# Idle products on TensorE ahead of the first h, the first two x tiles as one DMA, and the last output tiles in column halves

## Chip, cores and metric

The kernel runs on one core of a Trainium2 chip. The metric is the device time in microseconds; the median of 8 runs of the kernel before is 255.04 us (253.82 to 255.74). Lower is better.

## What is computed

One transformer block with adaptive layer norm (adaLN), for one sequence of 2048 positions, width 512, all in bfloat16:

```python
mod = silu(c) @ w_mod                       # six vectors of 512: sa, ca, ga, sb, cb, gb
h = layernorm(x) * (1 + ca) + sa
q, k, v = split(h @ wqkv)                   # 32 heads of 16
# sliding, dilated attention: position s sees s, s-2, ..., s-14 (8 keys)
logits = einsum('bhsd,bhswd->bhsw', q, k_gathered) * 16 ** -0.5
o = einsum('bhsw,bhswd->bhsd', softmax(logits), v_gathered)
x = x + ga * (o @ wo)
h = layernorm(x) * (1 + cb) + sb
x = x + gb * ((silu(h @ w1) * (h @ w3)) @ w2)   # w1, w3: 512 x 1792, w2: 1792 x 512
```

## The kernel before

The sequence is cut into 16 tiles of 128 positions, named T in the code. Everything stays in SBUF but v and the attention weights, which go to DRAM scratch and come back shifted, so that the eight neighbours of a position lie in one partition each.

The kernel does not write its instructions in order. It declares operations (`p.op`, `p.dma`), each with an engine, an estimated cost, a key into a table of priorities, and the values that it reads and writes. `schedule` then goes through time and gives each free engine the ready operation with the lowest priority value; buffers come from pools (8 PSUM banks, 5 of xn, 3 of h, 2 of pq, 2 of vsh and one more, vshx, on top of wqkv, 2 of o). The outcome is one fixed order for each engine, and `synchronize` puts semaphore waits where an operation depends on another engine. So each engine works through a list in order: where the head of a list waits, everything behind it on that engine waits too. Nearly all DMAs are issued from SP, in the order that the planner gave them, and cT alone from ScalarE.

The steps that the change and the prediction touch, with their lines in the profile:

- **Loads** (L133 for every DMA). x tiles 0 and 1 are two DMAs of 128 KB, then w_mod's first part (1 MB), then tiles 2 and 3 as two DMAs, then wqkv in three parts (q, k, v; 512 KB each) and the remaining x in groups of four tiles.
- **Modulation** (`modulation`, L522 to L531): 32 products of w_mod with silu(c), then three small VectorE operations give the scale and shift that the first h needs.
- **Layer norm** (`ln_stats`, L550 to L558): VectorE statistics (L550, L551), rstd on GpSimd in two operations (L553, L555), and the normalized tile xn on VectorE (L558).
- **h** (`ln_T`): TensorE transposes xn (L574, with the constant `ident`), and ScalarE (L582), in two early groups also VectorE (L589), applies scale and shift. Tiles are taken in the groups of `LN1` (2, 2, 4, 4, 4) for the first norm and of `FFN` (2, 4, 4, 4, 2) for the second.
- **Projections**: q and k transposed (`proj_qk`, L615), v (`proj_v`, L633); ScalarE evicts them (L622, L623, L643).
- **Attention**: VectorE forms all products q * k of a tile (`pq`, L664, 128x4096); TensorE sums them over each head with `E_sb` (L673); ScalarE takes exp (L687); VectorE normalizes (L699 to L710); the weights go through DRAM; VectorE multiplies the shifted v, `vsh`, by them (L733, 128x4096); TensorE sums over the neighbours with `ind` (L742); L755 multiplies by wo and L759 adds to x.
- **FFN** (`ffn_unit`): gate and up products (L771), Silu on ScalarE (L777), the product of both on VectorE (L780); `ffn_w2` sums 14 products with w2 (L792), L798 adds x, and a DMA stores the tile.
- **Constants**: GpSimd sets `ident`, `cst`, `ones` (L440), `E_sb` and the rest.

FFN work of early tiles fills TensorE while later tiles are in attention; the planner decides where.

Of the kernel before, what the change touches and what calls it, by code (L numbers as in the profile page):

```python
# [8 lines left out]
ALU = mybir.AluOpType  # L9
AX = mybir.AxisListType  # L10

P = 128
S = 2048
D = 512
# [5 lines left out]
NT = S // P  # L20
KT = D // P
NF = F // P
# [6 lines left out]
LAT = {"sp": 1900, "pe": 230, "dve": 70, "act": 150, "pool": 120}  # L29
DMA_RATE = 350  # L30
# [53 lines left out]
class Program:  # L84
# [41 lines left out]
    def dma(self, out, in_, key, nbytes, r=(), w=(), part=(), after=(), eng="sp", cost=450, group=None):  # L126
        nc = self.nc

        def fn(e):
            a = out() if callable(out) else out  # L130
            b = in_() if callable(in_) else in_
            with nc.allow_non_contiguous_dma(reason="layout"):
                return e.dma_start(a, b)  # L133

        o = self.op(eng, fn, cost, key, r=r, w=w, part=part, after=after, dma=nbytes)
        if group is not None:
            group.append(o)
            o.group = group
        return o

    def schedule(self, prio):
# [25 lines left out]
        while len(self.placed) < len(ops):  # L167
# [10 lines left out]
            for e in ENGINES:  # L178
# [31 lines left out]
                if o.dma:  # L210
                    dma_free = max(busy[e], dma_free) + o.bytes // DMA_RATE
                    o.end = dma_free + LAT["sp"]
                else:
                    o.end = busy[e] + LAT[e]
# [109 lines left out]
def c_dve(n):  # L324
    return 140 + n * 25 // 24
# [4 lines left out]
VG = 2  # L330
LN1 = [[0, 1], [2, 3], [4, 5, 6, 7], [8, 9, 10, 11], [12, 13, 14, 15]]
# [3 lines left out]
def _build(p, A_x, A_wqkv, A_wo, B_w1, B_w3, B_w2, c, w_mod, out):  # L335
# [67 lines left out]
    def bank(v):  # L403
        return PALL[:, v.at * 512:(v.at + 1) * 512]
# [28 lines left out]
    k = ("const", 0)  # L433
    p.op("pool", lambda e: e.memset(ident[:], 0.0), 150, k, w=[vident])
# [5 lines left out]
    p.op("pool", lambda e: e.memset(ones[:], 1.0), 150, k, w=[vc])  # L440
# [21 lines left out]
    p.dma(bass.AP(cT, 0, [[KT, P], [1, KT]]), bass.AP(c.tensor, c.offset, [[1, P], [P, KT]]), ("load", 0), 1024, w=[vcT],  # L462
          eng="act")
    for T in range(4):
        p.dma(x_sb[:, T, :], x_view[:, T, :], ("load", 1 if T < 2 else 19), 131072, w=[vx[T]])
    p.dma(wm_s[0][:], wm_view[:, :, 0:1024], ("load", 2), 1048576, w=[vwms[0]])
# [46 lines left out]
    def modulation(i):  # L513
# [17 lines left out]
        p.op("dve", lambda e: e.tensor_copy(modc[:, jlo:jlo + 8], modc_bf[:, jlo:jlo + 8]), 180, k, r=[vb16], w=[vmod[i]])  # L531

# [253 lines left out]
    def ffn_w2(T, tt, vhh):  # L786
        vz = Val("ps_z", psum)
        o = None
        for q in range(2):
            def mm(e, q=q):  # L790
                for fi in range(7 * q, 7 * q + 7):
                    ins = e.matmul(bank(vz), vhh[fi].at[:, tt * P:(tt + 1) * P], w2[:, fi, :], start=(fi == 0),  # L792
                                   stop=(fi == NF - 1))
                return ins

            o = p.op("pe", mm, 7 * MM, ("z", 2 * T + q), r=vhh[7 * q:7 * q + 7] + [vw2s], part=[vz], after=[o] if q else [])
        vo = Val("o", opool)
        p.op("dve", lambda e: e.tensor_tensor(vo.at[:], bank(vz), x_sb[:, T, :], ALU.add), c_dve(512), ("zo", T),  # L798
             r=[vz, vx[T]], w=[vo])
        finals.append(p.dma(out2d[T * P:(T + 1) * P, :], lambda: vo.at[:], ("zo", T), 131072, r=[vo], cost=400))  # L800

    modulation(0)
# [36 lines left out]
def _priorities():  # L839

    return {
        "ac": [-200350, -305143, -144949, -247454, -248998, -144926, 118091, 153034, 127660, 128134, 144119, -511708, -511789, 144159, 233884,
            140161],
        "ad": [-17874, -30405, -32779, -22500, -24840, -32434, -28265, -27668, 1469, -27769, 384, 367, 2705, 132755, -1479, -1613],
        "al": [-26059, -18199, -29495, -32976, -260310, -30646, -28356, -25679, -27023, -29130, 662, 915, 2008, 137184, 1131, 135573],
        "av": [-237126, -167739, 117729, 116760, 129499, 127502, -3576, 163212, 134914, 166331, 224073, 159673, 234283, 170474, 234369, 175760],
        "const": [-318511, -250028],
        "ex": [-152588, -142436, -140021, 53300, -139876, 74900, 96361, 96500, 96599, 118100, 127701, 139700, 124737, 182900, 182900, 182900],
        "f": [-13079, -234848, -103997, -152504, -114086, -145296, -116384, -248184, -248481, -146619, -145234, -198977, 121830, -31495, -146237,
            114050, 113238, 127970, 128137, 118188, 147491, -15588, -145226, 97902, 150981, -105983, -114355, 110896, 128277, 166736, 235566, 145004,  # L850
            129095, 111421, 199964, 125683, 128614, 162509, 159600, 129622, 140758, 180049, 222333, 160180, 163223, 238682, 226292, -511536, 159927,
            145684, -524879, 162898, 227475, 160131, -524977, 180052, 232502, 199837, 199314, -520876, -529180, 317000, 199316, 226185, 232431,
            -531683, 232315, 171522, 232311, 321759],
        "k": [-322297, -572741, -198760, -190131, -154342, -255908, -243988, -543578, -127644, -154350, -149316, -575519, -330997, -235009, -148795,
            -28906, -145161, -149323, -146794, -17610],
        "lg": [-150634, -142803, -233180, -327164, -249257, -235004, -259981, 127075, -199338, 128790, 139453, -31273, 113254, 140864, 118136,
            116232],
        "load": [99478, -565364, -558539, -275990, -275913, -291765, -289165, -25490, -17320, -28263, -14185, -289174, -261975, -5041, -260002,
            -17585, -261281, -30733, -17861, -296743],
        "mod": [-148763, -253150, -235125, -124038, -322327, -22533, -249983, -148006, 123104],  # L860
        "nm": [-1510043, -243017, -251504, -237638, -150689, -231747, -258507, -243906, -1114132, -232706, -250945, -254085, -250939, -247676,
            -248814, -240438, -234864, -234850, 126758, -146950, 130896, 140866, 168836, 126007, 134932, 122376, 159389, 164928, 225919, 126136,
            234809, 224413],
        "pq": [-252871, -156171, -145021, -250929, 127472, -240380, -243423, -244902, -109341, -239613, 169717, -108539, 134008, 133814, 125253,
            121981],
        "q": [-197716, -152472, -543562, -208803, -191857, -208358, -154375, -239569, -326610, -543026, -38787, -29129, -52704, -305134, -18763,
            106892, 113215, 91084, -141122, -151034],
        "rs": [-240379, -244702, 123968, -170661, -980, 135729, 175752, 128124, 163815, 128591, 122384, 227742, 128453, 133854, 128526, 159856],
        "sm": [-252811, -147149, -243616, 55300, 114437, 76900, -241462, 98500, -103045, 120100, 135088, 141700, 211236, 163300, 226628, 184900],
        "st": [-936849, -506834, -232582, 101744, -247943, -254078, -146807, -247930, -149835, -254071, -254208, -242818, -248804, -147329, -251009,  # L870
            -242935, -244460, -240797, 135436, 134779, 128454, -146248, 168855, 169729, 169974, 129804, 224348, 237239, 180639, 135109, 127857,
            238854],
        "tr": [98770, -253363, -208119, -243937, -192255, -188054, -56370, -256934, -138446, -189820, -122575, -31488, -152236, -146560, 140966,
            140158, 166028, 120267, 229725, -516185],
        "v": [-543494, -542831, -191851, -325240, -135881, -575945, -200493, -154170, 114839, -146400, -259983, 118127, -147068, -6268, -31482,
            -4183],
        "vl": [-289161, -291860, -261066, -265810, -34809, -37024, -29007, -32582, -261116, -24263, 1625, 137360, 2729, 821, 141175, -4774],
        "wo": [-170334, -145092, -198913, -198943, 103654, -121401, 120578, 117563, 157562, 139109, 145392, 202986, 159541, 129720, 233347, 205507],
        "z": [-152245, -145206, 96437, -198229, 144963, 117583, 135112, 113176, 150772, 140866, 128142, 128155, -515640, 227592, -512073, 145698,
            180068, -512484, -517177, 199975, 201180, -532961, 227954, -519840, 199333, -532793, 163756, 231059, 320680, 320620, 320078, 320681],  # L880
        "zo": [137033, -107703, 357, 175736, 2409, 221599, 169527, 164715, 159866, -553875, -657576, -553856, -558130, -657316, -691424, -708307],
    }
# [28 lines left out]
```

The softmax here doesn't subtract the row's maximum and nothing guards it: scores larger than these inputs give would overflow.

## Time and profile before

| Quantity | Value |
|---|---|
| median of 8 runs | 255.04 us (253.82 to 255.74) |
| the profiled execution's own time | 255.13 us |
| its span, first to last instruction | 253.4 us |
| TensorE busy (matmul) | 240.5 us, 95% |
| VectorE busy | 191.6 us, 76% |
| ScalarE busy | 111.5 us, 44% |
| GpSimd busy | 32.1 us, 13% |
| first product | at 5.62 us |
| first product on h (L633) | at 10.57 us |
| last product ends | about 250.5 us |

The span is the time between the first and the last instruction of the profiled execution; 1.73 us of its time lie around it. Busy time of an engine is the union of its instructions' durations. A matmul's shown duration includes its way through the array, so a 512-column product shows 379 ns where the next starts about 216 ns later: start-to-start times, or totals over many, are the ones to add. Groups are printed with line, engine, operation, output and input names, partitions x elements and count. A line of the waits reads: the engine and instruction that stood still, the one that released it, the sum, how often, and the longest.

### The profile page before, as it was taken

The page shows a single profiled execution, that of the slowest core. Times are in us where ns is not written, and L with a number is a line of the kernel's source. Part 1 is how long each engine was busy: PE and PEld are TensorE (multiplying, and loading weights), DVE is VectorE, ACT ScalarE, POOL GpSimd, SP SyncE. Part 2 cuts the span into 40 slices and gives each one's busy share as a digit, 9 for nine tenths or more (in the row PEclk, how much of TensorE's full clock was granted, in tenths as well). Part 3 has the DMA queues.
Part 4 walks back from the last instruction along what each step waited for, and adds up shares of the span by engine and source line. Part 5 has one row for each costly group of instructions (what it writes and reads, how often), then busy time and mean ns, then how long its engine had stood idle before and what let it go on. Part 6 is the DMA issues. An engine that isn't in the chain of part 4 may idle for free.

```text
span 253.4 us, 5507 instructions
## 1 busy us (share of the span) xinstructions
PE 240.5 (95%) x2296; PEld 140.1 (55%) x2296; DVE 191.6 (76%) x298; ACT 111.5 (44%) x198; POOL 32.1 (13%) x81
## 2 busy tenths in 40 slices
PE   0599989999999999999999999998999999999995
PEld 0368565655588666546654544645544444575572
DVE  4769889999998989999899899988952443431432
ACT  2169758964863358332561363333224332420120
POOL 6237541002000130000002200020030000000000
PEclk9999999999999999999999999999999999999999
DMA  5997999798875498322379145493001000000101
GB/s 192 359 325 199 290 326 351 195 330 267 233 178 147 131 280 220 62 25 62 109 225 271 45 104 85 115 286 102 1 0 44 0 0 21 21 3 21 41 23 41
DMA packets 45817, 36.29 MB, mean 143 GB/s; under 512 B 19408, under 2 KB 36576, under 8 KB 45792
## 3 DMA queue, kind: packets, MB, share of 16 engines
q1 hardware_dynamic: 45264, 35.94, 50.1%
q8 instruction: 18, 0.29, 0.5%
q10 hardware_dynamic: 528, 0.00, 0.1%
q14 instruction: 7, 0.06, 0.1%
HBM read 30.67 MB, written 5.26 MB: 142 GB/s over the span
## 4 chain that ended last, share of the span: by engine, by line
PE 85%; DMA 5%; DVE 5%; POOL 2%; SPq 1%; issue 0%
PE pall L771 36%; PE pall L792 19%; PE pall L615 9%; PE pall L633 5%; PE pall L755 5%; PE pall L742 4%; PE pall L673 4%; DMA sb_vsh<-v_scratch_dram 3%; DMA sb_x<-in_A_x_dram 2%; PE pall L574 2%; POOL sb_rs L555 1%; SPq L133 1%; DVE sb_xn L558 1%; DVE sb_st L550 1%; POOL sb_rs L553 1%; DVE sb_vsh L733 1%
## 5 line engine op out<-in xcount | busy, mean ns | idle before, releaser
L771 PE MATMUL pall<-sb_h,sb_w 128*128 128x512 bf16 (+1 forms) x560 | 101.7, 336 | 0.0
L771 PEld LDWEIGHTS pall<-sb_h,sb_w 128*128 128x128 bf16 x560 | 53.8, 98 | 41.2
L777 ACT ACTIVATE sb_sg<-pall 128x512 bf16<-128x512 f32 (+1 forms) x70 | 35.6, 511 | 70.6 <-PE pall L771 70.3
L780 DVE TENSOR_TENSOR sb_hh<-sb_sg,pall 128x512 bf16<-128x512 bf16 (+1 forms) x70 | 39.6, 578 | 26.0 <-PE pall L771 23.8
L792 PE MATMUL pall<-sb_w,sb_hh 128*128 128x512 bf16 x224 | 51.1, 379 | 0.0
L664 DVE TENSOR_TENSOR sb_pq<-sb_q,sb_kT 128x4096 bf16<-128x4096 bf16 x16 | 36.4, 2283 | 0.5 <-ACT sb_q L622 0.3
L792 PEld LDWEIGHTS pall<-sb_w,sb_hh 128*128 128x128 bf16 x224 | 21.5, 98 | 23.5 <-DVE sb_hh L780 0.2
L615 PE MATMUL pall<-sb_h,sb_wqkv 128*128 128x512 bf16 (+1 forms) x160 | 31.9, 340 | 0.0
L582 ACT ACTIVATE sb_h<-pall,sb_modc 128x512 bf16<-128x512 bf16 (+1 forms) x36 | 23.1, 708 | 18.8 <-PE pall L574 13.1
L733 DVE TENSOR_TENSOR sb_vsh<-sb_vsh,sb_al 128x4096 bf16<-128x4096 bf16 x12 | 27.3, 2284 | 1.4 <-DMA sb_vsh<-v_scratch_dram 1.4
L553 POOL TENSOR_TENSOR sb_rs<-sb_mv,sb_cst 128x1 f32<-128x1 f32 x32 | 8.9, 279 | 151.5 <-DVE sb_mv L551 148.5
L798 DVE TENSOR_TENSOR sb_o<-pall,sb_x 128x512 bf16<-128x512 f32 x16 | 11.0, 688 | 18.0 <-PE pall L792 18.0
L550 DVE BATCH_NORM_STATS2 sb_st<-sb_x 128x6 f32<-128x512 bf16 x32 | 21.8, 682 | 3.5 <-DMA sb_x<-in_A_x_dram 3.3
L555 POOL TENSOR_TENSOR sb_rs<-sb_rs,sb_cst 128x1 f32<-128x1 f32 x32 | 21.0, 655 | 2.5
L615 PEld LDWEIGHTS pall<-sb_h,sb_wqkv 128*128 128x128 bf16 x160 | 14.8, 99 | 10.8 <-ACT sb_h L582 0.7
L633 PE MATMUL pall<-sb_wqkv,sb_h 128*128 128x512 bf16 x64 | 17.8, 410 | 1.3 <-DVE sb_xn L558 1.3
L574 PE MATMUL pall<-sb_ident,sb_xn 128*128 128x128 bf16 x128 | 12.5, 224 | 6.4 <-DVE sb_xn L558 6.4
L673 PEld LDWEIGHTS pall<-sb_E,sb_pq 128*128 128x128 bf16 x512 | 14.7, 96 | 2.7 <-DVE sb_pq L664 0.6
L755 PE MATMUL pall<-sb_wo,sb_ot 128*128 128x512 bf16 x64 | 16.1, 379 | 0.0
L748 ACT ACTIVATE sb_ot<-pall 128x512 bf16<-128x512 f32 x16 | 9.6, 598 | 14.4 <-PE pall L742 14.4
L574 PEld LDWEIGHTS pall<-sb_ident,sb_xn 128*128 128x128 bf16 x128 | 9.4, 100 | 10.5 <-DVE sb_xn L558 6.9
L673 PE MATMUL pall<-sb_E,sb_pq 128*128 128x32 bf16 x512 | 15.1, 176 | 0.0
(59 smaller groups left out, 164.0 us busy)
## 6 DMA issues: line engine op xcount, KB each, us to landing
sb_vsh<-v_scratch_dram SPq DMA_DIRECT2D x48, 256.0 KB, 4.5
sb_vshx<-v_scratch_dram SPq DMA_DIRECT2D x16, 256.0 KB, 4.9
sb_wm_s<-in_w_mod_dram SPq DMA_DIRECT2D x2, 1024.0 KB, 6.7
v_scratch_dram<-sb_v SPq DMA_DIRECT2D x16, 128.0 KB, 5.6
sb_w<-in_B_w_dram SPq DMA_DIRECT2D x4, 512.0 KB, 8.6
out_dram<-sb_o SPq DMA_DIRECT2D x16, 128.0 KB, 1.7
sb_w<-in_B_w_dram SPq DMA_DIRECT2D x1, 1792.0 KB, 8.8
sb_wqkv<-in_A_wqkv_dram SPq DMA_DIRECT2D x3, 512.0 KB, 8.0
```

What stands on the lines that cost most here:

```text
L550: o = p.op("dve", lambda e: e.bn_stats(st[:, i, :], x_sb[:, T, :]), 670, k, r=[vx[T]], w=[vs])
L574: ins = e.transpose(b[:, col:col + P], vns[tt].at[:, ft * P:(ft + 1) * P], ident[:])
L615: ins = e.matmul(bank(vp)[:, 0:n], wqkv[:, t, col:col + P], vh.at[:, t, 0:n], start=(t == 0), stop=(t == KT - 1))
L633: ins = e.matmul(bank(vp), vh.at[:, t, tt * P:(tt + 1) * P], wqkv[:, t, 2 * D:3 * D], start=(t == 0), stop=(t == KT - 1))
L664: return e.tensor_tensor(vp.at[:], in0, in1, ALU.mult)
L673: ins = e.matmul(b[:, c0:c0 + H], vp.at[:, w, ft, :], E_sb[:, ft, :], start=(ft == 0), stop=(ft == KT - 1))
L733: return e.tensor_tensor(v_w, v_w, a_w, ALU.mult)
L755: ins = e.matmul(bank(vy), vt.at[:, ft, :], wo[:, ft, :], start=(ft == 0), stop=(ft == KT - 1))
L771: ins = e.matmul(bank(vp)[:, 0:n], wt[:, t, fi * P:(fi + 1) * P], vh.at[:, t, 0:n], start=(t == 0), stop=(t == KT - 1))
L777: p.op("act", lambda e: e.activation(vt.at[:, 0:n], bank(vgp)[:, 0:n], ACT.Silu), c_act(n), k, r=[vgp], w=[vt], table="silu")
L780: p.op("dve", lambda e: e.tensor_tensor(vh_.at[:, 0:n], vt.at[:, 0:n], bank(vup)[:, 0:n], ALU.mult), c_dve(n), k, r=[vt, vup], w=[vh_])
L792: ins = e.matmul(bank(vz), vhh[fi].at[:, tt * P:(tt + 1) * P], w2[:, fi, :], start=(fi == 0), stop=(fi == NF - 1))
```

## The change

Ahead of the first h, `warm(i)` adds 14 operations of five products each on TensorE: `ones` times `ones`, 128 x 128, into a PSUM bank whose content nobody reads. `ones` is set by VectorE, as its first instruction, and no longer by GpSimd. In the built order 50 such products come first on TensorE, 5 between the transposes of tile 0 and the modulation, and 15 after the transposes of tile 1.

x tiles 0 and 1 are loaded by one DMA; tiles 2 and 3 are also one DMA, declared after w_mod. In the built order SP issues x0-1, w_mod, x4-7, wv, wq, wk, x2-3, the zero row, x8-11, w_mod's gate part, wo, x12-15.

For tiles 14 and 15, `ffn_w2` forms the output in two halves of 256 columns: 14 products for each half, its own add (128x256) and its own store.

The planner's model is altered as well: a DMA that is not issued from SP no longer queues behind the others, cT and w_mod are given more bytes, and the whole table of priorities is new. With it, the order of all five engines differs from before nearly everywhere. `dma` gains a `transpose` argument that no call uses.

```diff
-                return e.dma_start(a, b)
+                return e.dma_start(a, b, transpose=True) if transpose else e.dma_start(a, b)
...
                 if o.dma:
-                    dma_free = max(busy[e], dma_free) + o.bytes // DMA_RATE
-                    o.end = dma_free + LAT["sp"]
+                    if e == "sp":
+                        dma_free = max(busy[e], dma_free) + o.bytes // DMA_RATE
+                        o.end = dma_free + LAT["sp"]
+                    else:
+                        o.end = busy[e] + 2 * o.bytes // DMA_RATE + LAT["sp"]
...
+NWARM = 14
...
+    p.op("dve", lambda e: e.memset(ones[:], 1.0), 150, k, w=[vc])
...
-    p.op("pool", lambda e: e.memset(ones[:], 1.0), 150, k, w=[vc])
...
-    p.dma(bass.AP(cT, 0, [[KT, P], [1, KT]]), bass.AP(c.tensor, c.offset, [[1, P], [P, KT]]), ("load", 0), 1024, w=[vcT],
+    p.dma(bass.AP(cT, 0, [[KT, P], [1, KT]]), bass.AP(c.tensor, c.offset, [[1, P], [P, KT]]), ("load", 0), 20000, w=[vcT],
           eng="act")
-    for T in range(4):
-        p.dma(x_sb[:, T, :], x_view[:, T, :], ("load", 1 if T < 2 else 19), 131072, w=[vx[T]])
-    p.dma(wm_s[0][:], wm_view[:, :, 0:1024], ("load", 2), 1048576, w=[vwms[0]])
+    p.dma(x_sb[:, 0:2, :], x_view[:, 0:2, :], ("load", 1), 262144, w=vx[0:2])
+    p.dma(wm_s[0][:], wm_view[:, :, 0:1024], ("load", 2), 1048576 + 200000, w=[vwms[0]])
+    p.dma(x_sb[:, 2:4, :], x_view[:, 2:4, :], ("load", 19), 262144, w=vx[2:4])
...
+    def warm(i):
+
+        vw = Val("ps_warm", psum)
+
+        def mm(e):
+            for _ in range(5):
+                ins = e.matmul(bank(vw)[:, 0:P], ones[:], ones[:], start=True, stop=True)
+            return ins
+
+        p.op("pe", mm, 535, ("warm", i), r=[vc], w=[vw])
...
     def ffn_w2(T, tt, vhh):
+
+        if T >= NT - 2:
+            n = D // 2
+            for q in range(2):
+                def mm(e, q=q, vz=Val("ps_z", psum)):
+                    for fi in range(NF):
+                        ins = e.matmul(bank(vz)[:, 0:n], vhh[fi].at[:, tt * P:(tt + 1) * P], w2[:, fi, q * n:(q + 1) * n],
+                                       start=(fi == 0), stop=(fi == NF - 1))
+                    return ins
+
+                vz = mm.__defaults__[1]
+                p.op("pe", mm, 7 * MM, ("z", 2 * T + q), r=vhh + [vw2s], w=[vz])
+                store(T, q * n, n, vz)
+            return
...
+        store(T, 0, D, vz)
+
+    def store(T, c0, n, vz):
         vo = Val("o", opool)
...
+        p.op("dve", lambda e: e.tensor_tensor(vo.at[:, 0:n], bank(vz)[:, 0:n], x_sb[:, T, c0:c0 + n], ALU.add),
+             c_dve(n), ("zo", T), r=[vz, vx[T]], w=[vo])
+        finals.append(p.dma(out2d[T * P:(T + 1) * P, c0:c0 + n], lambda: vo.at[:, 0:n], ("zo", T), 256 * n, r=[vo], cost=400))
+
+    for i in range(NWARM):
+        warm(i)
     modulation(0)
...
```

## The prediction

> **What bounds the kernel now.** I read the clock first (1.000 over the span, so nothing is throttled from outside), then busy time by engine, then what TensorE waits for, then its timeline at the start, the busy time by stage, and last the tail. TensorE's four waits (from, us, times, longest):
>
> ```profile
> PE pall L574 <- DVE sb_xn L558: 6.4, 2, 5.6
> PE pall L522 <- DMA sb_wm_s<-in_w_mod_dram: 1.6, 1, 1.6
> PE pall L633 <- DVE sb_xn L558: 1.3, 1, 1.3
> PE pall L742 <- DVE sb_vsh L733: 0.7, 1, 0.7
> ```
>
> They sum to 10.0 us of a 253.4 us span; another 2.9 us follow the last product. All but 1.4 us lies before 10.57 us: TensorE has nothing until the first x tile is normalized (5.6), then waits for w_mod (1.6), then for the first h (1.3). After that it stands still twice, 0.77 us at 36.91 and 0.66 us at 174.3. **But a busy TensorE need not be a fast one.** Its timeline (start, us, engine, line, count) has the same kind of product twice:
>
> ```profile
> 10.57 3.59 PE L633 MATMUL pall<-sb_wqkv,sb_h 128*128 128x512 bf16 x8 [1.28 <-DVE sb_xn L558]
> 13.96 1.04 PE L615 MATMUL pall<-sb_h,sb_wqkv 128*128 128x256 bf16 x4
> ...
> 175.11 2.75 PE L771 MATMUL pall<-sb_h,sb_w 128*128 128x512 bf16 x12
> ```
>
> Eight 512-column products hold it for about 3.4 us by their next start (0.43 each), where twelve later ones take 2.6 (0.216). The chain of waits gives the same: 3.59 for eight L633 and 0.83 for four L615, against 0.86 and 0.44 for four later ones. So the first twelve run at half speed, although the granted clock reads 1.00. They cost 3.59 - 1.73 = 1.86 and 0.83 - 0.44 = 0.39, **2.25 us**. Busy time by stage (PE, PEld, DVE, ACT, POOL):
>
> ```profile
> 10.57:15.00 4.43, 4.43 (x15) 1.98 (x16) 4.10 (x11) 1.19 (x2) 3.04 (x8) 1.00 1.10 348
> 15.00:41.00 26.00, 25.23 (x298) 17.29 (x296) 21.69 (x44) 19.63 (x41) 11.86 (x19) 1.00 0.96 289
> 41.00:95.00 54.00, 53.96 (x633) 34.79 (x631) 51.47 (x68) 32.98 (x61) 4.57 (x12) 1.00 0.81 227
> ...
> 183.00:250.50 67.50, 67.49 (x377) 36.20 (x375) 25.56 (x47) 18.45 (x36) 2.38 (x6) 1.00 0.05 16
> ```
>
> TensorE is the bound, but until 95 us VectorE is close behind it: idle 0.3 + 4.3 + 2.5 = 7.2 us of 84. From 183 us on it is mostly idle. What TensorE saves at the start must get past VectorE.
>
> **What the Trainium skill says.** (1) "TensorE: Matmul & The Clock Gate", What's actually happening: the array starts at half clock and is released by sustained activity, after a free-running window of about 3.4 us. The trace agrees: dense work from 10.57 is slow to 14.99 us, 4.4 us later. (2) "SBUF — State Buffer", SBUF: two separate sides: VectorE and GpSimd share a port pair under an exclusive lock, which a VectorE operation with two SBUF inputs takes against a GpSimd read. The trace agrees; the second row runs beside an L664 product:
>
> ```profile
> 25.69 0.55 POOL L555 TENSOR_TENSOR sb_rs<-sb_rs,sb_cst 128x1 f32<-128x1 f32 x1
> ...
> 26.74 2.70 POOL L555 TENSOR_TENSOR sb_rs<-sb_rs,sb_cst 128x1 f32<-128x1 f32 x1
> ```
>
> (3) "DMA: Bandwidth & Descriptors", Specifications: line rate needs 512 B or more in a row. Half an output row is exactly 512 B; no row of this trace shows that store.
>
> **The change part by part.**
>
> *x pair, and x2, x3 later.* SP issued x0, x1 (0.80 to 1.66), then w_mod at 1.70, which was used from 7.85. One issue of 0.43 fewer stands ahead of it, so w_mod and what hangs on it (32 L522 products, L528 to L531, two L582 and two L589) come 0.45 earlier: first h at 10.1. Bounds: -0.5, and +0.3, because the wv weights now sit behind 2.36 MB instead of 2.10. By the DMA rates by stage, wv landed at 9.9; 0.26 MB at 0.35 MB/us is +0.75, minus 0.45 is about 10.2. wq (11.6) and wk (13.1) follow, just when needed. Loading the pair as one DMA delays xn of tile 0 by some 0.4 us, hidden under w_mod, which is later. x2, x3 land at about 13.8, so x4 to x7 are normalized first.
>
> *70 idle products.* ones is set by VectorE first (0.2 us, ahead of a wait for x: nothing). 50 products at 107 ns (half speed, estimated as 128/512 of 0.43) fill 1.2 to 6.5; 5 and 15 more sit in the two later gaps. Transposes of tile 0 wait behind the 50, but w_mod is later still: 0 to +0.3, taken as 0. They hold the array busy over 5 us, more than the 4.4 it took, and no later gap reaches 2 us: -2.25.
>
> *Output halves.* Tiles 14, 15: 56 products of 256 columns at 0.109 replace 28 of 0.216: +0.05. After the last product came:
>
> ```profile
> 250.53 0.69 DVE L798 TENSOR_TENSOR sb_o<-pall,sb_x 128x512 bf16<-128x512 f32 x1 [0.82 <-PE pall L792]
> ```
>
> Half a tile costs 0.42, like the 256-wide L780: -0.27. Its store landed 1.7 us after issue; half the bytes I count as no gain. Two more SP issues of 0.33 each fall 1.5 us apart. Sum -0.22.
>
> *A new order.* Every priority changes, so all five orders do. The two old stalls (1.43) disappear as such and new ones come: this decides. I built both programs' orders and added, along each engine, the trace's start-to-start times (TensorE 0.216, 0.109, 0.056 by width, 0.79 per L673 or L742 block; VectorE 2.20 per L664 or L733, 0.82 per L550 with L551, 0.335 per L558, 0.61 or 0.36 per L780, and so on). This gives, at each handover, the earliest time of either engine if it never waits. TensorE counts from the first h, VectorE from the statistics next to it (before 10.57 and 10.46, after 10.1 and 9.8). Handovers, TensorE / VectorE earliest:
> - before: first L673 30.0 / 26.2; first L742 52.2 / 50.9; second 53.8 / 53.1; sixth 84.1 / 82.0.
> - after: first L673 29.8 / 29.4; fifth 41.2 / 41.0; second L742 58.5 / 58.2; sixth 87.0 / 86.7; twelfth L673 95.6 / 95.3. From 14 to 96 us most leads are 0.2 to 0.8, and about 20 us one is -0.4. From 139 us they are over 5.
>
> Test on before: at the transposes of 36.91 the lead is 0.9; TensorE was 2.15 late (cold), VectorE 4.0 late (its L664 at 33.47 stands at 29.5 in the sum); 0.9 + 2.15 - 4.0 = -0.95 against a measured stall of 0.77. So the new order hides nothing: **each us that VectorE waits, less about 0.3, becomes a stall of TensorE by 96 us.** Before, VectorE was 6.0 us late at 94 (L664 at 94.16). Part of that was waiting for TensorE itself (hh 0.9, x 0.6, h 2.2), which fades when it is the later engine; for GpSimd's rstd behind L664 it waited 1.2, for q 0.3. For after I take 1.5 for these, 0.5 at the h of tiles 2, 3 (its transposes queue behind banks that ScalarE frees), and 0.7 for hh and DMA: 2.7. Less 0.3, that is 2.4. From below: the h of tiles 4 to 7 needs about 8 evictions of 0.4 and four L582 of 0.72 on ScalarE, done at 18.7 when TensorE has only 7.4 us of work from 10.1, so at least 1.2. From above: 6.0 - 0.3 = 5.7. At 169 us vsh is freed 10.2 us before its next use, where the reload took 8.9 and L733 2.3 before: +0.1 (0 to 1.5). New stalls **2.5** (1.2 to 6).
>
> *Sum* against the profiled execution, 255.13 us (span 253.4 plus 1.73 around it, 0.09 above the median 255.04): -0.45 - 2.25 - 0.22 - 1.43 = -4.35; +2.5; = -1.85. 253.3, and 253.2 against the median.
>
> **The rivals.**
> (a) *VectorE as late as before (slower).* If it loses the same 6.0 us up to 96, TensorE stalls 5.7: -4.35 + 5.7 gives 256.5. It decides from stalls of 4.35 on (no change) or 5.1 (slower by 0.3%). For: leads under 0.8, and GpSimd still runs behind L664. Against: 3.7 of the 6.0 were waits for TensorE.
> (b) *The array doesn't stay warm.* The +2.25 returns, but a TensorE that is late has that much lead over VectorE, so stalls of 2.5 fall to about 0.3: again near 253.3. Alone it changes little; with w_mod no earlier, about 254.
> (c) *No new stall beyond ScalarE's 1.2:* 251.9. For: VectorE's waits for TensorE may vanish. Against: the one POOL row of 2.70.
> (d) *Gains cancelled:* stalls of 3.5 to 5, 254.3 to 255.8. For: the sum of small terms (DMA for wk, reloads of vsh, bank waits) has only upward errors.
>
> **How the numbers follow.** About 0.3%, 0.77 us, is what a measurement of this kernel can tell from no change. Likeliest case with (b) and (c): 0.63, faster. (d): 0.17, same. (a) and worse: 0.20, slower. Forecast 253.2, the likeliest case; range 251.5 (c, w_mod 0.4 earlier than thought) to 256.2 (near a); the likeliest alone 252 to 254.2.
>
> **What would show it.** In the profile after: eight first-h products at 0.216 from about 10.1; TensorE waits spread over 14 to 96 us on sb_xn, sb_pq and sb_vsh, in sum 1 to 3.5; VectorE over 95% busy there; the last DVE row 0.42. Wrong if TensorE's waits after 10 us stay under 1 or pass 4.5, if the first products take 0.43, or if a DMA for wqkv stands as the longest wait.

## The result, and the profile after

The changed kernel takes **256.88 us** (median of 11 runs, 256.55 to 258.74) against 254.96 us (median of 32 runs) of the kernel before: ratio **1.0097, interval 1.0076 to 1.0119**. It is slower by about 2 us, where I had forecast 253.2 and faster. The executions of the changed kernel lie in two groups, eight at 256.55 to 257.22 us and three at 258.49 to 258.74, so the medians differ by 1.9 us and the ratio, which weighs all of them, says 2.5. The profiled execution took 258.62 us (span 256.9, last instruction minus first), 1.7 above the median, so I read from it where the time goes, and from the runs how much. What TensorE waits for, in the form shown of before (engine and instruction, releaser, sum, times, longest):

```profile
PE pall L554 <- DMA sb_wm_g<-in_w_mod_dram: 2.0, 1, 2.0
PE pall L589 <- DVE sb_xn L573: 1.4, 1, 1.4
PE pall L543 <- DVE sb_ones L438: 1.1, 1, 1.1
PE pall L648 <- DVE sb_st L565: 1.0, 1, 1.0
PE pall L526 <- DVE sb_xn L573: 0.7, 1, 0.7
PE pall L808 <- DVE sb_hh L795: 0.6, 1, 0.6
```

7.0 us with the 0.2 us that a seventh line adds, where before had 10.0. **TensorE waits less and the kernel is slower**, so the sum of waits isn't the verdict. The longest is now a DMA: the gate part of w_mod (L554 was L539). L543 are the idle products, L648 the first products of h (L633 before), L589 the transposes (L574), L808 the output halves. The releaser named for L648 can't be right: that VectorE row is a statistic, which L648 doesn't read. What L648 reads came last with the wv weights, which landed at 11.11; in one of the experiments below (a_plain) their DMA is what is named. Next the timelines of TensorE and VectorE where they answer to those of before (start, us, engine, line, operation, count, idle time ahead of it):

```profile
4.58 0.69 DVE L565 BATCH_NORM_STATS2 sb_st<-sb_x 128x6 f32<-128x512 bf16 x1 [3.21 <-DMA sb_x<-in_A_x_dram]
...
11.24 3.46 PE L648 MATMUL pall<-sb_wqkv,sb_h 128*128 128x512 bf16 x8 [0.99 <-DVE sb_st L565]
14.54 2.35 PE L630 MATMUL pall<-sb_h,sb_wqkv 128*128 128x256 bf16 x20
...
21.09 1.71 PE L554 MATMUL pall<-sb_wm_g,sb_csb 128*128 128x512 bf16 x4 [2.01 <-DMA sb_wm_g<-in_w_mod_dram]
...
254.32 0.42 DVE L830 TENSOR_TENSOR sb_o<-pall,sb_x 128x256 bf16<-128x256 f32 x1 [1.10 <-PE pall L808]
```

The first x comes to VectorE at 4.58 instead of 3.15. The first h product is at 11.24 instead of 10.57, and the eight take 3.3 us to the next start (0.41 each): half speed, after all. The last row takes 0.42 as forecast. TensorE alone by stretches of that start (busy, count, granted clock, DMA share, GB/s):

```profile
1.12:5.54 4.42, 4.42 (x50) 1.00 0.46 124
5.54:11.05 5.51, 2.71 (x61) 1.00 1.08 373
11.05:14.45 3.40, 3.21 (x8) 0.50 1.10 352
14.45:21.09 6.64, 4.64 (x49) 1.00 1.12 286
21.09:24.70 3.61, 3.60 (x15) 0.53 0.31 101
```

The 50 idle products are done at 5.54, and then the array works for half of the time. The clock is taken back to 0.50 for about 3.4 us exactly when h is there, and again after the wait for the gate. Each such episode costs TensorE half its length. It need not cost the end: one execution with a mean granted clock of 0.986 took 256.55 us, and one with 1.000 took 256.81. By stages (PE, PEld, DVE, ACT, POOL, clock, DMA share, GB/s):

```profile
10.57:15.00 4.43, 3.76 (x13) 1.58 (x14) 3.98 (x11) 1.12 (x3) 3.02 (x8) 0.61 1.10 354
15.00:41.00 26.00, 23.99 (x230) 16.12 (x228) 19.88 (x42) 18.75 (x39) 7.85 (x20) 0.93 0.74 219
41.00:95.00 54.00, 53.85 (x764) 36.39 (x762) 52.65 (x62) 32.51 (x62) 6.21 (x6) 1.00 0.90 254
```

From 41 to 95 us, where I had expected the new stalls, TensorE is idle for 0.15 us. In this profile all the loss is ahead of 41.

One table from the timelines of seven kernels carries the rest: the first product of h, the first logits product, the end of the last VectorE row, and the difference of the last two.

| kernel | first h | first logits | last row ends | difference |
|---|---|---|---|---|
| before | 10.57 | 32.2 | 251.2 | 219.0 |
| b_pair | 11.37 | 33.8 | 253.4 | 219.6 |
| b_pe_plus | 10.84 | 33.2 | 252.8 | 219.6 |
| c_hold2 | 11.05 | 33.3 | 251.5 | 218.2 |
| after | 11.24 | 36.3 | 254.7 | 218.4 |
| a_plain | 10.86 | 33.5 | 252.3 | 218.8 |
| a_gate_late | 11.30 | 35.1 | 253.5 | 218.4 |

**Behind the first logits the new order is no longer than the old one.** Nor is it longer ahead of them by its work: by the prediction's sums TensorE has 19.7 us of it from the first h to the first logits after, and 19.4 before. So the new order's loss arises ahead of the first logits. Over all kernels below, the difference is 218.4 to 218.8 in the new order and 218.2 to 219.8 in the old one (b_best apart, with 222.1), one profile each: the table can't tell half a microsecond.

### The profile page after: what moved, and what is told of

The parts are those of the page before. It is cut to its first block, busy times and chain, and to the rows that moved or that the text cites. A ratio compares the mean times of both kernels' runs of the same rounds, so it can differ in the third digit from the quotient of the medians.

```text
span 256.9 us, 5706 instructions
## 1 busy us (share of the span) xinstructions
PE 247.2 (96%) x2394; PEld 148.5 (58%) x2394; DVE 191.8 (75%) x301; ACT 111.7 (43%) x198; POOL 30.8 (12%) x80
## 4 chain that ended last, share of the span: by engine, by line
PE 74%; DVE 14%; DMA 6%; issue 2%; POOL 1%; ACT 1%; SPq 0%; DVEq 0%
PE pall L786 38%; PE pall L821 16%; DVE sb_pq L679 7%; PE pall L770 5%; DMA sb_wm_g<-in_w_mod_dram 4%; PE pall L757 4%; PE pall L630 3%; PE pall L808 2%; PE pall L589 2%; DVE sb_vsh L748 2%; PE pall L648 2%; PE pall L688 2%; DMA sb_x<-in_A_x_dram 1%; ACT sb_h L597 1%; POOL sb_rs L568 1%
## 5 line engine op out<-in xcount | busy, mean ns | idle before, releaser
L795 DVE TENSOR_TENSOR sb_hh<-sb_sg,pall 128x512 bf16<-128x512 bf16 (+1 forms) x70 | 38.8, 575 | 25.0 <-PE pall L786 21.6
L821 PE MATMUL pall<-sb_w,sb_hh 128*128 128x512 bf16 x196 | 45.2, 379 | 0.0
L679 DVE TENSOR_TENSOR sb_pq<-sb_q,sb_kT 128x4096 bf16<-128x4096 bf16 x16 | 36.3, 2282 | 0.0
L630 PE MATMUL pall<-sb_h,sb_wqkv 128*128 128x512 bf16 (+1 forms) x160 | 30.7, 336 | 0.0
L821 PEld LDWEIGHTS pall<-sb_w,sb_hh 128*128 128x128 bf16 x196 | 18.9, 98 | 20.0
L830 DVE TENSOR_TENSOR sb_o<-pall,sb_x 128x512 bf16<-128x512 f32 (+1 forms) x18 | 11.2, 629 | 18.5 <-PE pall L821 13.4
L570 POOL TENSOR_TENSOR sb_rs<-sb_rs,sb_cst 128x1 f32<-128x1 f32 x32 | 19.9, 621 | 2.5
L648 PE MATMUL pall<-sb_wqkv,sb_h 128*128 128x512 bf16 x64 | 17.6, 419 | 1.0 <-DVE sb_st L565 1.0
L573 DVE TENSOR_SCALAR sb_xn<-sb_x,sb_mv,sb_rs 128x512 bf16<-128x512 bf16 x32 | 12.3, 402 | 3.0 <-PE pall L589 1.3
L757 PEld LDWEIGHTS pall<-sb_ind,sb_vsh 128*128 128x128 bf16 x384 | 11.3, 96 | 2.6 <-issue 0.4
```

Of the source, the lines that this page charges most:

```text
L630: ins = e.matmul(bank(vp)[:, 0:n], wqkv[:, t, col:col + P], vh.at[:, t, 0:n], start=(t == 0), stop=(t == KT - 1))
L648: ins = e.matmul(bank(vp), vh.at[:, t, tt * P:(tt + 1) * P], wqkv[:, t, 2 * D:3 * D], start=(t == 0), stop=(t == KT - 1))
L679: return e.tensor_tensor(vp.at[:], in0, in1, ALU.mult)
L795: p.op("dve", lambda e: e.tensor_tensor(vh_.at[:, 0:n], vt.at[:, 0:n], bank(vup)[:, 0:n], ALU.mult), c_dve(n), k, r=[vt, vup], w=[vh_])
```

## The experiments

Names with a_ start from the changed kernel, b_ and c_ from the kernel before. In all of them the order of every engine was kept as built and only what the diff shows was moved, added or removed; where a kernel in the old order gets idle products, `ones` is set by VectorE there too, and in a_plain it stays there. Each ratio is to runs of the kernel before on the same chip and session (medians 255.14 to 255.30 us).

### First: which part of the change

**a_gate_late.** The gate products, their eviction and the scaling of wo are moved behind later work.

```diff
 PE:  k1
-PE:  gate (L554)
 PE:  transposes of tiles 2, 3; v5, k9, v6
+PE:  gate (L554)
```

> The kernel after with only the gate product moved: four L554 products, their eviction and the scaling of wo stand later in the orders of TensorE, ScalarE and VectorE (behind the v products of the first h of tiles 4 to 7), the loads stay as they are. Theory A (loads): the 2.0 us wait for w_mod's gate part and the half clock after it (about 1.8 us) set TensorE back ahead of the transposes of tiles 2 and 3, and VectorE with it. The wait goes, TensorE is 2 to 4 us earlier at the first L688, and the time falls from 256.9 to about 254.5. Theory B (VectorE): the new order holds VectorE so tight that it sets the end whatever TensorE waits for in the first 22 us; the time falls by 0.4 at most.

Measured: 257.81 us, ratio 1.0101 (1.0080 to 1.0121). The wait is gone from the list and nothing is gained. What TensorE meets instead, all by 26 us, is xn, h and the evicted gate:

```profile
PE pall L589 <- DVE sb_xn L573: 0.9, 2, 0.7
PE pall L630 <- ACT sb_ga_bc L559: 0.8, 1, 0.8
...
PE pall L648 <- ACT sb_h L597: 0.7, 1, 0.7
```

So the longest wait was not the cause; the next ones were right behind it.

**a_x_two.** x0 and x1 are loaded by two DMAs again.

```diff
-SP:  x0-1 (256 KB)
+SP:  x0 (128 KB), x1 (128 KB)
 SP:  w_mod
```

> The kernel after with x tiles 0 and 1 as two DMAs again, in the place of the one, nothing else. Theory A (loads): x0 lands at about 3.2 us and not at 4.55, cT's and w_mod's landings move back towards those of before, the first product on h comes at about 10.6 and not at 11.24, and the time falls by about 0.6. Rival: the late landing comes from the two queues and the loads behind, not from the size of the first DMA; x0 lands after 4 us, and the time is the same within 0.3.

Measured: 256.64 us, 1.0072 (1.0047 to 1.0097). The point estimate is 0.6 us better than after's, but the intervals overlap. The first h was expected at 10.6 and came at 11.28, no earlier than after's 11.24: wv landed at 11.14 here too. And the run tests little of the pair. x0 landed at 3.13, but the new table of priorities puts tile 1 first on VectorE, and x1 landed at 4.22:

```profile
4.25 0.69 DVE L565 BATCH_NORM_STATS2 sb_st<-sb_x 128x6 f32<-128x512 bf16 x1 [2.88 <-DMA sb_x<-in_A_x_dram]
```

That is 0.33 us ahead of the 4.58 of the changed kernel, where the old order gained 1.4.

**a_no_warm.** The idle products are taken out.

```diff
-PE:  50 idle products
 PE:  transposes of tile 0
-PE:  5 idle products
 PE:  w_mod; transposes of tile 1
-PE:  15 idle products
 PE:  first h products (L648)
```

> The kernel after without its 70 idle products, all orders else as they are. Theory A: the clock that they gain is lost again ahead of the first h (half clock from 11.05 to 14.45 us in the profile after), so without them the first twelve products are as slow as now, and the time is the same within 0.4. Rival (the idle products pay): the time rises by 1 to 2 us. Second rival (they harm, by standing ahead of the transposes or by the clock falling twice): it falls by 0.5 or more.

Measured: 256.94 us, 1.0062 (1.0041 to 1.0083). Without its main part the changed kernel is no slower. The wait for w_mod's gate part is gone too (the reason stands under "Fourth"). The first h products take as long without idle products as with them:

```profile
11.25 3.57 PE L648 MATMUL pall<-sb_wqkv,sb_h 128*128 128x512 bf16 x8 [1.57 <-DVE sb_st L565]
14.62 3.32 PE L630 MATMUL pall<-sb_h,sb_wqkv 128*128 128x256 bf16 x20
```

**b_halves.** The kernel before with the output halves alone.

```diff
-PE:  per tile 7 hh x 512 columns, 7 hh x 512 columns
+PE:  per half 14 hh x 256 columns
```

> The kernel before with only the last two tiles' output in halves of 256 columns. As predicted in the sum: -0.22 us (-0.27 for the shorter last add, +0.05 for the products). Rival: each half now waits for all 14 hh before its first product where a group of seven did before, which showed as a wait of 0.6 us in the profile after: +0.3 to +0.4 us.

Measured: 255.75 us, 1.0017 (1.0002 to 1.0031): slightly slower. The first half needs all 14 hh, where the whole tile began with seven, and TensorE waits for the last of them:

```profile
PE pall L793 <- DVE sb_hh L780: 0.6, 1, 0.6
```

### Second: edits against order

**b_all** puts all three edits into the old order, **a_plain** undoes all three in the new one.

```diff
 b_all                              a_plain
-SP: x0, x1, w_mod, x2, x3          -SP: x0-1, w_mod ... x2-3
+SP: x0-1, w_mod, x2-3              +SP: x0, x1, w_mod ... x2, x3
+PE: 50, 5, 15 idle products        -PE: 50, 5, 15 idle products
+tiles 14, 15 in halves             -tiles 14, 15 in halves
```

> The three named edits (70 idle products, x0-1 and x2-3 as one DMA each, the last two tiles in column halves) in the order of the kernel before, which is otherwise kept instruction for instruction. Theory 'order' (the re-planned order carries most of the 1.9 us): 255.0 to 255.9 us, that is the +0.4 us of the halves and little else. Theory 'edits' (the pair that lands later and the clock that is lost again carry it): 256.5 to 257.2, as the changed kernel. The forecast's own reckoning for the same edits (-4.35 us without new stalls) would give 251 to 252.5.

> The order of the changed kernel, with all three named edits undone: no idle products, x0, x1, x2, x3 as four DMAs at the same places of the queue, the last tiles' output whole. Theory 'order': 256.2 to 256.9 us, slower than the kernel before by 1.0 to 1.7 us although both then hold the same instructions. Theory 'edits': 255.0 to 255.5, no different from the kernel before.

Measured: b_all 256.61 us, 1.0062 (1.0046 to 1.0077); a_plain 256.33 us, 1.0036 (1.0019 to 1.0053). Neither theory alone: both halves cost, and 0.62% + 0.36% = 0.98% is the 0.97% of the whole. a_plain holds the same instructions as before and differs by its order alone (and by `ones` on VectorE, 0.17 us while it waits for x). TensorE's waits there show where:

```profile
PE pall L648 <- DMA sb_wqkv<-in_A_wqkv_dram: 1.5, 1, 1.5
PE pall L648 <- ACT sb_h L597: 0.8, 1, 0.8
```

wv is loaded behind x4 to x7 now, and h of tiles 4 to 7, taken ahead of tiles 2 and 3, is not ready when TensorE has run out of tiles 0 and 1. Before had no wait at all between 10.57 and 36.9. These two are read from the waits; no run here takes one of them back alone.

**a_hold** and **b_hold** keep the array busy up to the first h, in the new and in the old order.

```diff
 a_hold                             b_hold
-PE: 50, 5, 15 idle products        (none before)
+PE: 72, 16, 31 idle products       +PE: 50, 34, 24 idle products
```

> The changed kernel with 49 more idle products where TensorE waits ahead of the first h: 22 more before the first transposes, 11 more before the products with w_mod, 16 more before the first products of h. Theory 'clock' (what was lost is the half speed of the first h, since the array had idled from 5.5 us on): the clock stays at 1.00 through 14 us, the eight first products take 0.216 us each, and 1.5 to 2 us come off the end: about 255.0. Theory 'given back': the clock stays high but the time goes into a longer wait for w_mod's gate columns, which land at 21 whatever TensorE does (3.5 to 4 us instead of 2.0), and the end moves by less than 0.5: 256.4 to 257.2.

> The kernel before, order kept, with idle products alone, enough to fill TensorE's waits up to the first h: 50 before the first transposes, 34 before the products with w_mod, 24 before the first products of h. Theory 'clock': the first h at full speed from 10.6 us on, 2 us off the end: 253.0 to 253.5. Theory 'given back' (VectorE and the transfers set when the next h and the first logits come): TensorE reaches them earlier and waits there, 254.8 to 255.5, within 0.2% of the kernel before.

Measured: a_hold 257.60 us, 1.0087 (1.0057 to 1.0117); b_hold 254.97 us, 0.9993 (0.9982 to 1.0005). In both "given back" is nearer, though a_hold's median lies above the 257.2 expected: five of its twelve executions show a mean clock of 0.993 and took 258.2 us and more, the other seven took 256.7 to 257.8 (median 256.8, like the changed kernel). The array stays warm in a_hold's profile (same columns as above):

```profile
5.54:11.05 5.51, 5.51 (x115) 1.00 1.08 371
11.05:14.45 3.40, 3.40 (x29) 1.00 1.10 356
```

and in the same profile the lead goes here:

```profile
13.11 1.47 PE L630 MATMUL pall<-sb_h,sb_wqkv 128*128 128x256 bf16 x12
15.39 1.05 PE L630 MATMUL pall<-sb_h,sb_wqkv 128*128 128x256 bf16 x8 [0.81 <-DMA sb_wqkv<-in_A_wqkv_dram]
...
21.07 1.02 PE L554 MATMUL pall<-sb_wm_g,sb_csb 128*128 128x512 bf16 x4 [2.43 <-DMA sb_wm_g<-in_w_mod_dram]
```

The gate products start at 21.07; in the changed kernel they started at 21.09.

### Third: who has slack

Four kernels in the old order: **b_pair** has only the pairs of x; **b_dve_plus** adds 1.38 us of VectorE work, **b_pe_plus** 1.4 us of TensorE work; **b_best** was my candidate for a version better than both.

```diff
 b_pair                b_dve_plus                b_pe_plus                   b_best
-SP: x0, x1            DVE: h of tiles 0, 1      PE: k2                      +PE: 50, 20, 24 idle products
+SP: x0-1             +DVE: 2 x statistics x0   +PE: 25 idle products        -DVE: scaling of wo (L811)
 SP: w_mod             DVE: xn of tile 2         PE: gate (L539)             +POOL: scaling of wo, at 40 us
-SP: x2, x3
+SP: x2-3
```

> The kernel before, order kept, with only the pairs: x0 and x1 as one DMA, x2 and x3 as one DMA, at the places of the first of each. Theory 'VectorE' (VectorE and the x that it waits for set the pace up to the feed-forward): its first statistics start 1.4 us later, the whole of its row shifts, and the end with it: 256.2 to 256.5 us, +1.2. Theory 'TensorE' (only TensorE's own row counts): w_mod lands 0.3 to 0.4 us later and with it the first h: 255.4 to 255.6.

> The kernel before, order kept, with two more statistics rows (of 0.69 us each, 1.38 in all, over x0 again, results unused until they are overwritten) on VectorE right after its part of the first h, ahead of the normalisation of tile 2. Nothing else changes. Theory 'VectorE' and theory 'both' (neither engine has slack): 256.2 to 256.6 us, nearly the whole 1.38 at the end. Theory 'TensorE': 255.2 to 255.6.

> The kernel before, order kept, with 25 idle products (0.056 us each at full clock, 1.4 in all) on TensorE ahead of the gate products, at 17.5 us, behind the transposes of tiles 2 and 3. Theory 'VectorE': TensorE takes the delay out of slack, 255.2 to 255.6 us. Theory 'TensorE' and theory 'both': 256.1 to 256.6.

> The kernel before, order kept, with idle products (50, 20 and 24) that keep the array warm up to the first h, and with the scaling of wo by the gate (1.22 us on VectorE at 22 us) moved to GpSimd, which idles from 40.6 to 61.6 us. Theory 'VectorE': 253.8 to 254.2 us, the 1.2 us of the scaling come off the end. Theory 'both': TensorE's 0.9 to 1.7 us from the full clock and VectorE's 1.2 us count only together, 253.9 to 254.5. Theory 'TensorE': as with the idle products alone, 254.8 to 255.3. What could spoil it: GpSimd holds VectorE back while it scales wo, then 255 to 257.

Measured:

| kernel | median us | ratio (interval) |
|---|---|---|
| b_pair | 256.20 | 1.0035 (1.0018 to 1.0053) |
| b_dve_plus | 255.60 | 1.0013 (0.9997 to 1.0030) |
| b_pe_plus | 257.65 | 1.0092 (1.0062 to 1.0123) |
| b_best | 258.12 | 1.0121 (1.0094 to 1.0149) |

My theory that VectorE sets the pace falls for the old order: 1.38 us more on it, at 10 us, can't be told from nothing (at most 0.8 us by the interval), while 1.4 us more on TensorE, at 17 us, cost all of it and more. (2.3 us by the ratio, over nine runs from 255.4 to 258.4; the profile shows 1.6 at the last row, 0.3 of it from a first h that came later, and what the rest is stays open.) TensorE has no slack there. b_pair, which with b_halves makes 0.52% of b_all's 0.62%, costs what it delays the first h, 0.8 us, and a little more:

```profile
8.89 0.69 DVE L551 BATCH_NORM_STATS2 sb_st<-sb_x 128x6 f32<-128x512 bf16 x1 [0.57 <-DMA sb_x<-in_A_x_dram]
...
9.71 0.13 DVE L529 CAST sb_modc_bf<-pall 128x8 bf16<-128x8 f32 x1
...
11.37 1.03 PE L634 MATMUL pall<-sb_wqkv,sb_h 128*128 128x512 bf16 x2 [1.68 <-DVE sb_xn L559]
```

In the kernel before these stand at 8.09, 8.92 and 10.57:

```profile
8.09 0.69 DVE L550 BATCH_NORM_STATS2 sb_st<-sb_x 128x6 f32<-128x512 bf16 x1 [1.15 <-DMA sb_x<-in_A_x_dram]
...
8.92 0.13 DVE L528 CAST sb_modc_bf<-pall 128x8 bf16<-128x8 f32 x1
```

The first pair's lateness is hidden: the first transposes come 1.37 us later, and TensorE still waits 0.65 us for w_mod after them. Two other things are not. w_mod lands at 8.11 and not at 7.71; and x2-3 land at 8.86, where x2 alone came at 8.07, and on VectorE the statistics of tile 2 stand ahead of the modulation that the first h needs. (The releaser named for the first h, xn, is not what it reads.)

b_best failed for a reason of its own. GpSimd's scaling and one VectorE row, from the timelines of both:

```profile
38.38 0.42 DVE L710 TENSOR_TENSOR sb_attn<-sb_ex,sb_ssum 128x256 bf16<-128x256 f32 x1
...
40.49 4.05 POOL L811 TENSOR_TENSOR sb_wo<-sb_wo,sb_ga_bc 128x2048 bf16<-128x2048 bf16 x1
40.71 4.12 DVE L710 TENSOR_TENSOR sb_attn<-sb_ex,sb_ssum 128x256 bf16<-128x256 f32 x1
```

The same L710 takes 0.42 us without GpSimd and 4.12 beside it. The Trainium skill has it in "SBUF — State Buffer", Who interferes with whom: a VectorE operation with two SBUF inputs and a GpSimd operation that reads SBUF exclude each other, and whoever issues first holds the other up. The expectation named this as what could spoil it, at 255 to 257; 258.12 is more than that.

### Fourth: why a warm array brings nothing

**c_hold2** is b_hold without the delay that its 34 products caused. **c_load0** loads wq ahead of x4 to x7, **c_load1** does so with a warm array, **c_load2** moves wk there as well.

```diff
 c_hold2: +PE: 50, 20, 24 idle products
 c_load0                    c_load1: c_load0 and             c_load2: c_load1 and
 SP: wv                     +PE: 50, 20, 24 idle products     SP: wv, wq
+SP: wq                                                      +SP: wk
 SP: x4-7                                                     SP: x4-7
-SP: wq                                                      -SP: wk
+DVE: xn of tile 3 ahead of the statistics of tile 5
```

> The kernel before, order kept, with 50, 20 and 24 idle products: the array is warm at the first h without delaying the products with w_mod. Theory 'transfers': TensorE has the first eight products done by 12.4 us and then waits 1 to 1.7 us for wq, so nothing is left at the end: 254.8 to 255.3 us. Theory 'clock': 253.0 to 253.6.

> The kernel before with wq loaded ahead of x4 to x7, and the normalisation of tile 3 on VectorE ahead of the statistics of tile 5; no idle products. Both theories: the first h still runs at half speed and does not need wq before 14 us, so nothing is gained; x4 to x7 land about 1.5 us later, of which VectorE's slack takes most: 255.1 to 256.0.

> As c_load0, with 50, 20 and 24 idle products. Theory 'transfers': TensorE no longer waits for wq at 12.4 us but for wk at about 15.2 or, later, for VectorE; 0.3 to 1 us is left at the end: 254.1 to 254.8. If VectorE's slack is used up by the later x4 to x7: 255.0 to 255.5.

> As c_load1, with wk ahead of x4 to x7 as well. Theory 'transfers': no wait of TensorE for wq or wk; x4 to x7 land at about 15 us, and the question is whether VectorE catches up: 253.8 to 254.6 if it does, 255.5 to 256.5 if its later row then ends last (TensorE's waits for xn after 20 us of 1 us and more).

Measured: c_hold2 255.23 us, 1.0000 (0.9986 to 1.0014); c_load0 255.18, 1.0003 (0.9988 to 1.0019); c_load1 255.10, 1.0005 (0.9983 to 1.0026); c_load2 256.06, 1.0051 (1.0030 to 1.0073). In c_hold2 the eight first products run at full speed (one record of them is missing), and the gain stands in the next bracket:

```profile
11.05 1.67 PE L633 MATMUL pall<-sb_wqkv,sb_h 128*128 128x512 bf16 x7 [0.48 <-ACT sb_h L582]
14.39 0.61 PE L615 MATMUL pall<-sb_h,sb_wqkv 128*128 128x256 bf16 x4 [1.67 <-DMA sb_wqkv<-in_A_wqkv_dram]
```

With wq first (c_load1) TensorE passes 12.43 without a wait and stands at 15.35 for wk:

```profile
15.35 1.05 PE L615 MATMUL pall<-sb_h,sb_wqkv 128*128 128x256 bf16 x8 [1.22 <-DMA sb_wqkv<-in_A_wqkv_dram]
```

With both first (c_load2) it passes these too and stands here:

```profile
PE pall L539 <- DMA sb_wm_g<-in_w_mod_dram: 1.4, 1, 1.4
PE pall L615 <- DVE sb_h L589: 1.3, 1, 1.3
```

From 5.5 to 14.5 us the DMAs move 350 to 370 GB/s without a pause (the stretches above; before shows 348), and a warm TensorE uses each load about when it lands. In the three orders of the loads tried here, a faster TensorE meets the next load, or the VectorE work that hangs on one. No version beat the kernel before.

But the loads did not stand still. A load reports in sixteen parts, and who waits for it waits for the last of them. Landing times in us, from the traces:

| kernel | idle products ahead of the first h | first 16 KB packet of instructions | wq | wk | gate part of w_mod | its last part behind the other fifteen |
|---|---|---|---|---|---|---|
| before | none | 20.52 | 12.95 | 14.45 | 15.97 | 0.14 |
| b_pair | none | 21.81 | 13.37 | 14.88 | 16.39 | 0.05 |
| b_hold | 108 | 11.81 | 13.00 | 15.16 | 16.68 | 0.70 |
| c_hold2 | 94 | 12.00 | 14.35 | 15.86 | 17.37 | 1.31 |
| a_no_warm | none | 21.54 | 12.62 | 14.13 | 18.16 | 0.10 |
| after | 70 | 12.67 | 12.61 | 15.48 | 20.96 | 2.76 |

In all ten kernels with idle products ahead of the first h the queue named "instruction" moves its first 16 KB packet at 11.7 to 12.8 us, and from the next loads on one part in sixteen comes late; in all eight without them it moves at 20.5 to 21.8. From 12 to 20 us the last part of some load falls back by 0.4 to 1.4 us more than that of the load ahead of it where there are idle products, and by 0.2 at most where there are none. The gate part, from issue to landing, in a_no_warm and then in the changed kernel:

```profile
DMA to landing us min/median/max: 8.7/8.7/8.7
DMA to landing us min/median/max: 11.5/11.5/11.5
```

So the 2.0 us wait of the changed kernel goes with the idle products and not with the order, and the wait for wq in c_hold2 is long because wq came 1.4 us later than before. That the added instructions have to be fetched, and that their packet holds up one of the sixteen ways, is my reading; no run here has a warm array with fewer instructions. What a warm array would bring with the loads as they land in the kernel before is therefore not shown: wq was there 1.0 us ahead of its first use at 13.96, so at that point 1.0 of the 1.66 us that the eight products lose could have passed.

## Why the prediction was wrong

**Step "x pair": -0.45 forecast, about +0.9 measured (b_pair 0.35%).** The step that failed is "one issue fewer ahead of w_mod, so it comes 0.45 earlier". w_mod was indeed issued 0.39 us earlier (1.31 against 1.70), but it landed at 8.09 and not at 7.71, and its products started at 8.23 instead of 7.85. The pair itself landed 3.75 us after its issue, where x0 alone took 2.33, so the first xn came 1.27 us later, not "some 0.4"; that this would be hidden under w_mod was right. In the old order the pair of x2 and x3 adds the rest (b_pair). In the new order the first h waits for wv, forecast for 10.2 and landed at 11.11, with one DMA or two (a_x_two 11.14). I had priced an issue on the queue, and not the transfer.

**Step "70 idle products": -2.25 forecast, nothing measured.** It failed in three places. First, "no later gap reaches 2 us" was no reason for the clock to hold: three gaps of 1.35, 0.65 and 0.99 us between 5.5 and 11.2 were enough to lose it. That was rival (b). Second, the term counts TensorE's time as the end's. Its size was nearly right (from start to start the first twelve products lost 1.66 and 0.41, or 2.07; 1.73 for eight products when warm is right), but a_hold, b_hold and c_hold2 have the warm array and no gain: TensorE then waits for loads. A part of the 2.07 was hidden under the load of wq in the kernel before: I estimate 0.65, since warm products from 10.57 would be done at 12.30 and wq landed at 12.95. Before showed no wait there because TensorE was slow enough never to wait; I took "busy" for "bound". Third, the idle products were taken to cost 0, with +0.3 at most, and only by holding up transposes; with them loads after 12 us landed up to 2.8 us later (the gate part, 20.96 against 18.16). How the lost gain divides between the second and the third, no run here tells. Rival (b)'s own reasoning, that a late TensorE would only lose its lead over VectorE, is refuted, for the old order, by b_pe_plus.

**Step "output halves": -0.22 forecast, 0.17% (0.4 us) slower in the old order.** The row of 0.42 was right; what I left out is that a half waits for all 14 hh. In the new order the whole tile waits 0.6 us too (a_plain), and there the difference in the table is 0.4 us less with halves; one profile each, so not more than a hint.

**Step "a new order": stalls of 2.5 forecast, in place of 1.43.** The order alone costs 0.36% (a_plain), 0.9 us; that the forecast's 1.1 us is near is luck, for most of its content did not come. Its stalls were to come from VectorE's leads of 0.2 to 0.8 between 14 and 96 us. Against its never-waiting sum TensorE is 6.5 us late at the first logits (36.3 against 29.8) and 7.4 at the twelfth (103.0 against 95.6), so it loses 0.9 between them. The 6.5 add up from the start: 1.1 for the first h, 1.7 for each of two stretches at half speed, 2.0 for the gate part. What the order itself adds is read from a_plain: wv behind x4 to x7, landed at 10.72 against 9.94, and 0.85 us for the h of tiles 4 to 7, which the prediction did have, as "at least 1.2". The loads it had mis-sized: wv, wq and wk at 10.2, 11.6 and 13.1, "just when needed", landed at 11.11, 12.61 and 15.48 in the changed kernel.

**The rivals.** Rival (a) gave 256.5, near the result, but by VectorE's lateness; b_dve_plus shows that VectorE has slack in the old order. In the new one that was not tested: the chain that ended last in its profile runs from the gate part through VectorE's products between 36 and 67 us, where TensorE's work is all but without a gap. Of my signs, "first products at 0.43" came true (0.41), and a DMA did stand as the longest wait, though for w_mod and not for wqkv. All rivals shared the fault: each weighed engines against each other, and gave the loads small terms at most.

## What to carry to other kernels

Where a kernel starts while its weights are still arriving, write down beside each engine's row when each load lands; a gain on an engine ends at the next landing, and a wait that isn't in the list may only be hidden by slowness. Compare the landings of both versions as well: filler work that costs its engine nothing may come with later loads. Ask of each engine in both directions: add a microsecond to it (b_pe_plus, b_dve_plus) to see whether it has slack, and take one away (c_hold2) to see who is next; here no version of the kernel before gained. Taking away the longest wait of a profile (a_gate_late) proves nothing until the end moves.

## What I had not expected of the hardware

- A gap of 2.0 us in TensorE's work cost the clock in the changed kernel (0.53 from 21.09 to 24.70), while a gap of 2.43 us at the same place in a_hold did not (1.00). The Trainium skill, "TensorE: Matmul & The Clock Gate", Why this matters for your kernels, advises against gaps over about 3 us; here shorter ones in a row were enough. Its section What's actually happening has a free-running window of about 3.4 us, and the records fit it: in the changed kernel the granted clock changes at 11.05, 14.46, 21.29 and 24.70 us, which is in steps of 3.41 or twice that.
- The half-speed start from a cold array stands as clock 1.00 in the views, the fall after work as 0.50: the first clock record of the kernel before begins at 14.84, with 1.00, and the time ahead of it has none. In both the eight products take about 3.4 us.
- One DMA of 256 KB for x0 and x1 landed 3.75 us after its issue, the two of 128 KB 2.33 and 3.02 after theirs. From 1.12 to 5.54 us the DMAs moved 124 GB/s, against some 350 later.
- Work that an engine does in its idle time can come with late loads: with 70 idle products the gate part of w_mod landed at 20.96, without them at 18.16 (a_no_warm), one of its sixteen parts 2.76 us behind the rest.
